# An S4 convolution block on one core: K's transform kept by contiguous channels, and two FFT stages turned through DRAM

## The chip, the cores and the metric

The kernel runs on one core of a Trainium2 chip. The metric is the device time of one execution in microseconds. Engines are named as in the profile: PE (TensorE matmul), PEld (its weight load), DVE (VectorE), ACT (ScalarE), POOL (GpSimd) and SP (SyncE, which issues most DMAs).

## What is computed

```python
mod = (silu(c) @ w_mod).reshape(1, 6, 1, 512)
sa, ca, ga, sb, cb, gb = (mod[:, i] for i in range(6))
h = layernorm(x) * (1 + ca) + sa                  # x: (1, 2048, 512)
x = x + ga * s4(h)                                # long convolution along the sequence
h = layernorm(x) * (1 + cb) + sb
x = x + gb * (mish(h @ w1 + b1) @ w2)             # 512 -> 1792 -> 512

def s4(u):
    P = exp((dt * A)[:, :, None] * arange(2048))  # A: (512 channels, 128 states), complex
    K = einsum("dn,dnl,dn->dl", C, P, dt * B).real
    y = irfft(rfft(u padded to 4096) * rfft(K padded to 4096))[:2048]
    return y + u * Dskip
```

Everything is float32. The feed-forward part runs as products of high and low parts, three matmuls for one.

## The kernel before

**The convolution as two-stage transforms.** The 2048 rows of the sequence are read as 128 x 16 (a partition holds 16 consecutive rows, index j), the 512 channels as four blocks b of 128. A transform has an outer stage (small matrices bdk, bdu for the input, di for the way back) and an inner stage (128 x 128 matrices mf forward, mi back, 32 of them). Both are matmuls, and between the stages data has to be turned, since a matmul contracts over partitions. A block's work is cut into eight groups v = 8b + s; 32 groups in all.

**The K branch** makes the convolution kernel for 16 channels per group. Angles (`s_ang`, one two-bank PSUM tile `pang`), rounding (`s_ri`) and its subtraction on PE (`s_neg`), sine and cosine (`s_sin`) and magnitudes (`s_mag`, L377, L380) meet in `s_comb` on DVE (L387 to L391); `s_kgen` multiplies them on PE (L402), `s_ks` adds the skip term, `s_ka` runs the outer stage (weights ks, moving bdk, L418) and `s_tm` copies it to the one tile `gk` (L426), in an order of channels that differs between even and odd blocks. `s_ubk` takes its weights from gk with a stride (L546, tile `pkb`): for a fixed group and r, neighbouring channels are 16 or 128 bytes apart.

**The u branch** per block: `h_slice` loads the block's rows again and normalises them on ACT (L512; block 0 uses the rows `XR` that are already in SBUF); `ua` runs the outer stage with h's slices as weights and bdu as the moving operand (L526), so channels come out on partitions, and scales by 1 + ca (L528, `modp[:, 3]`); `s_ut` turns them with PE transposes (L536) and copies to `gu` (L538); `s_ubu` runs the inner stage with gu as weights and adds the shift sa (rows `sab`, made by `shift_mm` and `shift_rows`) through a short bf16 matmul (L553); `s_ug` scales by ga (L563).

**Product and way back.** `s_prod` multiplies both spectra on DVE, channels on partitions (L583 to L585); `s_t1` transposes (L590, L592); `s_invb` runs the inner inverse with the data as weights (L601) and copies scattered to `z` (L603); `s_t2` transposes z (L611) into `zt` (L614); `s_inva` runs the outer inverse with the constant di as weights (L637), adds x (`s_xp` loads it) and stores to `x2d` in DRAM (L640).

**Order.** The work is a software pipeline over slots k = -1 to 40. `ORDER` lists the steps with an offset: a step with offset o does group k - o in slot k. `UD` adds a further offset per group to ua, ut, ubu and ug. `MS`, `SL` and `HS0` place the modulation vectors, parameters and row slices; `PRI0` and `PRI` move steps within a slot. From these priorities each engine gets a fixed instruction order; engines are in order and wait on each other by semaphores. SP's queue is in order as well: a DMA that waits for a buffer holds up those behind it. At slot 34 the generator's memory is released and w1 loaded (`mlp_open`), at the end the second layer norm (`ln_stats`, `ln_norm`, `ln_t`) hands over to the feed-forward loop (L897, L915).

Of the kernel before, what the change touches and what calls it, by code (L numbers as in the profile page):

```python
# [30 lines left out]
SL = {"p2": 0, "p3": 2, "ls0": 5, "raw": 2, "p0": 5, "ls1": 8, "co0": 6, "vis": 6, "h0": -5, "h1": -2}  # L31
HA = 4
NUG = 2
MS = [[3, 0], [5, 2], [0, 4], [1, 6], [2, 8], [4, 9]]
BN = [0, 0, 0, 1]
NS = 1
HS0 = [2, 3, 3, 2]
# [9 lines left out]
UD = [4, 4, 3, 3, 2, 3, 3, 3, 3, 3, 3, 3, 3, 3, 3, 4, 4, 4, 4, 4, 4, 4, 4, 4, 4, 4, 4, 4, 4, 4, 4, 4]  # L47
# [7 lines left out]
def _constants():  # L55
# [34 lines left out]
    for e in range(3):  # L90
# [12 lines left out]
        "bdk": bdk.reshape(P, 256).astype(f),  # L103
        "bdu": np.ascontiguousarray(bdu).reshape(P, 256).astype(f),
        "di": np.ascontiguousarray(di.transpose(1, 2, 3, 0, 4, 5)).reshape(P, 256).astype(f),
# [7 lines left out]
def _channels():  # L113

    d = np.arange(NB * P).reshape(NB, P)
    return np.stack([d[b].reshape(8, 2, 8).transpose(1, 0, 2) if b % 2 == 0 else
                     d[b].reshape(2, 8, 8).transpose(0, 2, 1) for b in range(NB)])
# [3 lines left out]
def s4_block(ctx, tc, io, out):  # L121
# [290 lines left out]
    def s_ka(k):  # L412
        p = bank("pka")
        PKA[k] = p
        for m in range(4):
            o = 256 * (m % 2) + 128 * (m // 2)
            for cc in range(2):
                T.matmul(p[64 * cc:64 * cc + 64, o:o + 128], KS[k][:, 64 * m:64 * m + 64],  # L418
                         bdk[:, 128 * cc:128 * cc + 128], start=True, stop=True)

    def s_tm(k):
        b, c = divmod(k, 8)
        if k == 0:
            GK[0] = big.tile([P, 8, 16, 8, 4], F32, tag="gk", name="gk")
        dst = GK[0][:, c] if b % 2 == 0 else GK[0][:, :, :, c, :].rearrange("p s d e -> p d s e")
        A.copy(dst, PKA[k].rearrange("p (d s e) -> p d s e", d=16, s=8))  # L426
# [5 lines left out]
    modp = keep.tile([P, 5, NB], F32, name="modp")  # L432
# [4 lines left out]
    mcol = gen.tile([P, 20, KB], F32, name="mcol", bufs=1)  # L437

    def mod_load(n):
        s, k = divmod(n, KB)  # L440
        w = cv.tile([P, D], F32, tag="zt", name=f"wm{n}", bufs=4)
        nc.sync.dma_start(w, w_mod((2, 3, 4, 1, 5, 0)[s] * D, D, k))
        WM[n] = w
# [19 lines left out]
    PM = []  # L463

    def shift_mm(k):
        if k == 0:
            PM.append(bank("pmod"))
        T.matmul(PM[0], sc[:, k:k + 1].to_broadcast([P, P]), WM[20 + k], start=(k == 0), stop=(k == KB - 1))

    def shift_rows():  # L470
        p = PM[0]
# [6 lines left out]

# [19 lines left out]
    HS, XP, U1, GU, YY, YT, Z, ZT = {}, {}, {}, {}, {}, {}, {}, {}  # L498

    def h_slice(b, part):  # L500
        if part == 0:
            HS[b] = sl8(f"h{b}").rearrange("p (j d) -> p j d", j=16)
            if b > 0:
                for j4 in range(4):
                    x_rows(HS[b][:, 4 * j4:4 * j4 + 4], 4 * j4, 4, b)
            return
        h = HS[b]
        bs = slice(b * P, b * P + P)
        for jj in range(4 * (part - 1), 4 * part):
            src = XR[jj][:, bs] if b == 0 else h[:, jj, :]  # L510
            if jj % 4 < HA:
                A.activation(h[:, jj, :], src, AF.Identity, scale=rstd[:, jj:jj + 1], bias=nmr[:, jj:jj + 1])  # L512
            else:
                V.tensor_scalar(h[:, jj, :], src, mv[:, jj, 0:1], rstd[:, jj:jj + 1],
                                op0=OP.subtract, op1=OP.mult)

    def s_ua(n):
        for j4 in ((0,), (1,), (2, 3), ())[n % 4]:
            ua(n // 8, n % 8 // 4, j4)

    def ua(b, rp, j4):
        if j4 == 0:
            U1[b, rp] = cv.tile([P, 8, 16, 16], F32, tag="u1", name=f"u1_{b}_{rp}")
        p = bank("pua")
        for jj in range(4):
            T.matmul(p[:, 128 * jj:128 * jj + 128], HS[b][:, 4 * j4 + jj, :],  # L526
                     bdu.rearrange("p (a r) -> p a r", r=32)[:, :, 16 * rp:16 * rp + 16], start=True, stop=True)
        A.mul(U1[b, rp][:, :, 4 * j4:4 * j4 + 4, :].rearrange("p a j r -> p j a r"),  # L528
              p.rearrange("p (j a r) -> p j a r", j=4, a=8), modp[:, 3, b:b + 1])

    def s_ut(v):
        b, s = divmod(v, 8)
        u = U1[b, s // 4].rearrange("p a j r -> p (a j) r")
        p = bank("put")
        for r in range(4):
            T.transpose(p[:, P * r:P * r + P], u[:, :, 4 * (s % 4) + r], ident)  # L536
        GU[v] = cv.tile([P, 4, P], F32, tag="gu", name=f"gu{v}")
        A.copy(GU[v].rearrange("p r d -> p (r d)"), p)  # L538
# [463 lines left out]
```

## Time and profile before

| | us |
|---|---|
| median of three runs | 763.28 |
| lowest and highest | 763.0, 764.53 |
| span of the profiled execution | 758.2 |
| PE busy, of the span | 707.0 |
| DVE busy | 450.6 |
| ACT busy | 428.3 |
| first feed-forward matmul (L897) at | 437.9 |

The span runs from the first to the last instruction; the runs' times also hold what lies around it, and no time outside the span is given for the profiled execution itself. A PE record is one pass of a matmul: a float32 matmul of the convolution part leaves two. Busy times of groups overlap, because matmuls are pipelined, so that groups add up to more than PE's busy time in a window; the chain that ended last counts each moment once.

### The profile page before, as it was taken

The page shows a single profiled execution, that of the slowest core. Times are in us where ns is not written, and L with a number is a line of the kernel's source. Part 1 is how long each engine was busy: PE and PEld are TensorE (multiplying, and loading weights), DVE is VectorE, ACT ScalarE, POOL GpSimd, SP SyncE. Part 2 cuts the span into 40 slices and gives each one's busy share as a digit, 9 for nine tenths or more (in the row PEclk, how much of TensorE's full clock was granted, in tenths as well). Part 3 has the DMA queues.
Part 4 walks back from the last instruction along what each step waited for, and adds up shares of the span by engine and source line. Part 5 has one row for each costly group of instructions (what it writes and reads, how often), then busy time and mean ns, then how long its engine had stood idle before and what let it go on. Part 6 is the DMA issues. An engine that isn't in the chain of part 4 may idle for free.

```text
span 758.2 us, 14266 instructions
## 1 busy us (share of the span) xinstructions
PE 707.0 (93%) x5888; PEld 587.0 (77%) x5888; DVE 450.6 (59%) x918; ACT 428.3 (56%) x689; POOL 52.4 (7%) x108
## 2 busy tenths in 40 slices
PE   0794999999999999999998789999999999999997
PEld 0562879987888898889888568888888888888885
DVE  6889798799899969984464487119211521143113
ACT  3767798989999998776664254233222322232221
POOL 1006203310060200000000000000000000000000
PEclk9987899999999999999999899999999999999999
DMA  9653224200241101110460362002200220002001
GB/s 312 237 194 77 63 66 116 48 8 10 58 112 57 43 2 43 57 57 2 148 215 28 97 187 65 0 1 92 75 1 1 81 87 1 0 1 84 0 1 55
DMA packets 47096, 52.70 MB, mean 70 GB/s; under 512 B 7221, under 2 KB 32825, under 8 KB 46265
## 3 DMA queue, kind: packets, MB, share of 16 engines
q1 hardware_dynamic: 40312, 47.93, 19.6%
q0 software_dynamic: 6720, 3.87, 2.7%
q8 instruction: 46, 0.75, 0.4%
q14 instruction: 18, 0.14, 0.1%
HBM read 41.30 MB, written 8.39 MB: 66 GB/s over the span
## 4 chain that ended last, share of the span: by engine, by line
PE 84%; DVE 7%; ACT 5%; DMA 2%; issue 1%; POOL 0%; SPq 0%; DVEq 0%; ACTq 0%; POOLq 0%
PE pm L897 20%; PE po L915 20%; PE pkb L546 8%; PE pka L418 4%; PE pub L546 4%; PE pua L526 4%; PE pib L601 4%; PE pkg L402 4%; PE pia L637 3%; PE put L536 2%; PE pang L344 2%; PE pang L362 2%; PE pmodp L448 2%; PE pt L611 2%; PE pt L590 2%; ACT ec L145 1%
## 5 line engine op out<-in xcount | busy, mean ns | idle before, releaser
L145 ACT ACTIVATE mh<-pm,b 128x512 f32<-128x512 f32 x56 | 38.6, 690 | 200.0 <-PE pm L897 200.0
L904 DVE TENSOR_TENSOR mal<-mh,mah 128x512 fp32r<-128x512 f32 x56 | 38.7, 691 | 177.6 <-ACT mah L903 177.3
L897 PE MATMUL pm<-hh,w1h 128*128 128x512 f32 x448 | 139.1, 393 | 2.8 <-ACT hh L803 2.8
L897 PEld LDWEIGHTS pm<-hh,w1h 128*128 128x128 f32 x448 | 84.5, 189 | 21.6 <-ACT hh L803 3.5
L915 PE MATMUL po<-w2h,mah 128*128 128x512 f32 x224 | 87.9, 392 | 0.0
L897 PE MATMUL pm<-hh,w1l 128*128 128x512 f32 x224 | 87.5, 392 | 0.0
L915 PE MATMUL po<-w2l,mah 128*128 128x512 f32 x224 | 87.5, 391 | 0.0
L915 PE MATMUL po<-w2h,mal 128*128 128x512 f32 x224 | 87.5, 390 | 0.0
L583 DVE TENSOR_TENSOR q<-pkb,ug 128x512 f32<-128x512 f32 x64 | 41.2, 685 | 47.4 <-PE pkb L546 47.3
L546 PE MATMUL pkb<-mf,gk 128*128 128x128 f32 x256 | 63.3, 389 | 0.2
L546 PEld LDWEIGHTS pkb<-mf,gk 128*128 128x128 f32 x256 | 60.6, 318 | 1.8 <-ACT gk L426 0.5
L603 ACT COPY z<-pib 128x512 f32<-128x512 f32 x32 | 35.1, 1098 | 33.7 <-PE pib L601 33.7
L897 PEld LDWEIGHTS pm<-hh,w1l 128*128 128x128 f32 x224 | 42.5, 190 | 8.8
L915 PEld LDWEIGHTS po<-w2h,mal 128*128 128x128 f32 x224 | 42.1, 188 | 8.6
L915 PEld LDWEIGHTS po<-w2h,mah 128*128 128x128 f32 x224 | 42.1, 188 | 8.4
L915 PEld LDWEIGHTS po<-w2l,mah 128*128 128x128 f32 x224 | 42.1, 188 | 8.2
L387 DVE TENSOR_TENSOR ec<-ec,m 128x1024 f32<-128x1024 f32 x32 | 38.9, 1216 | 9.8 <-ACT ec L145 9.8
L402 PE MATMUL pkg<-ec 128*32 128x64 f32 x2048 | 40.8, 228 | 0.5 <-DVE ec L388 0.3
L526 PE MATMUL pua<-bdu,h 128*128 128x128 f32 x256 | 37.5, 286 | 3.2 <-ACT h L512 3.2
L402 PEld LDWEIGHTS pkg<-ec 128*32 128x32 f32 x2048 | 34.4, 112 | 7.3 <-issue 2.2
L418 PE MATMUL pka<-bdk,ks 128*64 128x128 f32 x512 | 39.5, 289 | 0.1
L377 DVE TENSOR_TENSOR m<-co 128x1024 f32<-128x1024 f32 x32 | 38.9, 1216 | 0.1
(167 smaller groups left out, 1322.5 us busy)
## 6 DMA issues: line engine op xcount, KB each, us to landing
wm<-in_w_mod SPq DMA_DIRECT2D x24, 256.0 KB, 3.1
xr<-in_A_u SPq DMA_DIRECT2D x4, 1024.0 KB, 12.9
out<-ot SPq DMA_DIRECT2D x16, 256.0 KB, 2.0
xp<-in_A_u SPq DMA_DIRECT2D x15, 256.0 KB, 3.0
x2d<-xp SPq DMA_DIRECT2D x15, 256.0 KB, 2.4
xt<-x2d SPq DMA_DIRECT2D x15, 256.0 KB, 4.5
w1s<-in_B_w SPq DMA_DIRECT2D x8, 448.0 KB, 4.0
w2s<-in_B_w SPq DMA_DIRECT2D x14, 256.0 KB, 2.9
```

Of the source, the lines that this page charges most:

```text
L145: chain(A.activation(out, in_, f, **kw))
L377: V.tensor_mul(m2.rearrange("p d (a b) -> p d a b", a=8), co[:, :, 12:20, None].to_broadcast([P, 16, 8, 8]), co[:, :, None, 20:28].to_broa ...
L387: V.tensor_mul(ec[:, :, :, 32:64], ec[:, :, :, 95:63:-1], m2[:, None, :, 0:32].to_broadcast([P, 2, 16, 32]))
L402: T.matmul(o, ec[:, z, e, 0:32], ec[:, z, e, 32:96], start=(z == 0), stop=(z == 1))
L418: T.matmul(p[64 * cc:64 * cc + 64, o:o + 128], KS[k][:, 64 * m:64 * m + 64], bdk[:, 128 * cc:128 * cc + 128], start=True, stop=True)
L526: T.matmul(p[:, 128 * jj:128 * jj + 128], HS[b][:, 4 * j4 + jj, :], bdu.rearrange("p (a r) -> p a r", r=32)[:, :, 16 * rp:16 * rp + 16], s ...
L546: T.matmul(pv[:, :, r, :], lh(r), mf[:, 4 * s + r, :].rearrange("p (c s) -> p c s", c=2), start=not started, stop=True, skip_group_check=s ...
L583: V.tensor_mul(q, kv[:, c, :, None, :].to_broadcast([P, 4, 2, 64]), ug)
L603: A.copy(Z[b, hf][:, :, :, o:o + 4].rearrange("p j a r -> p r a j"), p.rearrange("p (r a j) -> p r a j", r=4, a=8))
L897: T.matmul(p, w1[wi][:, k, fs], hh[:, hi, k, :], start=(n == 0), stop=(n == 3 * KB - 1))
L904: V.tensor_sub(a[1], h, a[0])
L915: T.matmul(PO[tt][q], a[ai][:, P * q:P * q + P], w2[wi][:, f, :], start=(f == 0 and n == 0), stop=(f == FB - 1 and n == 2))
```

## The change

- `s_ka` writes its result with r outside and four channels inside, into places that interleave the 16 channels; `s_tm` copies them so that `gk` holds, for every r, 128 contiguous channels. There is one gk tile per block now, odd and even blocks in different memory. `bdk` and the order of channels on the host (`_channels`) follow.
- The outer input stage runs once for all channels, early (slots 1 to 4): DVE normalises the rows in place, 512 channels at a time (`norm`, 16 of them); `ua` takes the constant bdu as weights and a row group as the moving operand, 512 columns, 16 j x 2 halves. ACT copies to a staging tile, and pairs of j are stored to a DRAM tile `ud`. `s_gl` loads a group's `gu` from there, turned, in place of `s_ut`. The second read of the rows (`h_slice`) goes.
- The factor 1 + ca moves behind the stage: `s_ug` scales by gd = ga (1 + ca), and the shift is divided by 1 + ca (`shift_ratio`). The shift's rows come from a column form, made like the other modulation vectors, and four small broadcast matmuls.
- `s_invb` takes the constant mi as weights and the data as the moving operand; the result is copied contiguously and stored to DRAM tiles `zd`; `s_zl` loads it back turned, in place of the transposes of `s_t2`.
- `UD` goes; offsets, some buffers' tags and the places of the modulation vectors change. Tiles `gu` and the modulation weights share four buffers; `us` stages both ud and z in two.

```diff
-SL = {..., "vis": 6, "h0": -5, "h1": -2}
-MS = [[3, 0], [5, 2], [0, 4], [1, 6], [2, 8], [4, 9]]
+SL = {..., "vis": 6}
+MS = [[3, 0], [5, 1], [0, 3], [1, 6], [2, 8], [4, 9]]
+MR = 5
-UD = [4, 4, 3, 3, 2, ...]
 ORDER = [
-    ("kgen", 1), ("ks", 1), ("ubu", 3), ("ang", -2), ("ua", -1), ("hs", 0), ("ri", -2), ("misc", 0),
-    ("t2", 13), ("mag", -1), ("t1", 9), ("ka", 1), ("par", 0), ("tm", 1), ("neg", -2), ("ut", 2),
-    ("comb", 0), ("ubk", 8), ("inva", 13), ("ug", 4), ("xp", 10), ("sin", -2), ("invb", 9), ("prod", 8),
+    ("kgen", 1), ("ks", 1), ("ubu", 7), ("ang", -2), ("gl", 6), ("ri", -2), ("misc", 0), ("zl", 13),
+    ("mag", -1), ("t1", 9), ("ka", 1), ("par", 0), ("tm", 1), ("neg", -2),
+    ("comb", 0), ("ubk", 8), ("inva", 14), ("ug", 7), ("xp", 13), ("sin", -2), ("invb", 9), ("prod", 8),
 ]
...
     def s_ka(k):
+        pv = p.rearrange("p (r d) -> p r d", d=16)
         for m in range(4):
-            o = 256 * (m % 2) + 128 * (m // 2)
+            o = 8 * (m % 2) + 4 * (m // 2)
             for cc in range(2):
-                T.matmul(p[64 * cc:64 * cc + 64, o:o + 128], KS[k][:, 64 * m:64 * m + 64],
+                T.matmul(pv[64 * cc:64 * cc + 64, :, o:o + 4], KS[k][:, 64 * m:64 * m + 64],
                          bdk[:, 128 * cc:128 * cc + 128], start=True, stop=True)

     def s_tm(k):
-        dst = GK[0][:, c] if b % 2 == 0 else GK[0][:, :, :, c, :].rearrange("p s d e -> p d s e")
-        A.copy(dst, PKA[k].rearrange("p (d s e) -> p d s e", d=16, s=8))
+        if c == 0:
+            GK[b] = (cv if b % 2 else big).tile([P, 32, P], F32, tag="gk", name=f"gk{b}", bufs=1)
+        A.copy(GK[b][:, :, 16 * c:16 * c + 16], PKA[k].rearrange("p (r d) -> p r d", d=16))
...
+    def shift_ratio():
+        d = modp[:, 3, :]
+        V.tensor_scalar(gd, d, 0.0, 1e-20, op0=OP.is_equal, op1=OP.mult)
+        V.tensor_add(d, d, gd)
+        V.tensor_mul(gd, modp[:, 0, :], d)
+        V.reciprocal(d, d)
+        V.tensor_mul(modp[:, 5, :], modp[:, 5, :], d)
...
     def shift_rows():
+        for b in range(NB):
+            T.matmul(p[:, b * P:b * P + P], modp[:, 5, b:b + 1].to_broadcast([P, P]), ident, start=True, stop=True)
...
+    def norm(j):
+        V.tensor_scalar(XR[j], XR[j], mv[:, j, 0:1], rstd[:, j:j + 1], op0=OP.subtract, op1=OP.mult)
+
+    def ua(j, hf):
+        if j % 2 == 0:
+            US[j // 2, hf] = cv.tile([P, NB, 2, P], F32, tag="us", name=f"us{j}{hf}", bufs=2)
+        t = US[j // 2, hf]
         p = bank("pua")
+        T.matmul(p, bdu[:, P * hf:P * hf + P], XR[j], start=True, stop=True)
+        A.copy(t[:, :, j % 2, :], p.rearrange("p (b d) -> p b d", b=NB))
+        if j % 2:
+            nc.sync.dma_start(view(ud, hf * NB * P * SEG + (j - 1) * P, [[SEG, P], [P * SEG, NB], [1, 2 * P]]),
+                              t.rearrange("p b j d -> p b (j d)"))
+
+    def s_gl(v):
         b, s = divmod(v, 8)
+        GU[v] = cv.tile([P, 512], F32, tag="gu", name=f"gu{v}", bufs=4).rearrange("p (r d) -> p r d", r=4)
+        nc.sync.dma_start(GU[v], view(ud, (s // 4 * NB + b) * P * SEG + 4 * (s % 4) * 8 * SEG,
+                                      [[P, P], [8 * SEG, 4], [1, P]]))
...
     def s_ubk(v):
+        kr = lambda r: GK[b][:, 4 * s + r, :]
...
     def s_invb(v):
         for r in range(4):
-            T.matmul(p[:, P * r:P * r + P], YT[v][:, r, :], mi[:, 4 * s + r, :], start=True, stop=True)
+            T.matmul(p[:, P * r:P * r + P], mi[:, 4 * s + r, :], YT[v][:, r, :], start=True, stop=True)
+        z = cv.tile([P, 4, P], F32, tag="us", name=f"z{v}", bufs=2)
+        A.copy(z, p.rearrange("p (r d) -> p r d", r=4))
+        nc.sync.dma_start(view(zd[b][s // 4], 4 * (s % 4) * 8 * SEG, [[P, P], [8 * SEG, 4], [1, P]]), z)
+
+    def s_zl(y):
+        ZT[b, j4] = cv.tile([P, 2, 512], F32, tag="x4", name=f"zt{b}{j4}", bufs=3)
+        for hf in range(2):
+            nc.sync.dma_start(ZT[b, j4][:, hf, :].rearrange("p (j d) -> p j d", j=4),
+                              zd[b][hf][:, 4 * j4:4 * j4 + 4, :])
...
+    at(MR, shift_ratio)
+    at(MR, shift_rows)
...
+    for n, j in enumerate((12, 13, 14, 15, 8, 9, 10, 11, 0, 1, 2, 3, 4, 5, 6, 7)):
+        at(NS, norm, j)
+        for hf in range(2):
+            at(NS + n // 4, ua, j, hf)
```

More of the change, by code (lines that the diff above doesn't have):

```diff
@@ L497, in s4_block @@
     LNX, LST = {}, {}
[L498 to L523, printed above, removed]
-        p = bank("pua")
[L525 to L529, printed above, removed]
@@ L531, in s_ut @@
-    def s_ut(v):
-        b, s = divmod(v, 8)
[L533 to L538, printed above, removed]
+    XP, GU, YY, YT, ZT, US = {}, {}, {}, {}, {}, {}
+    SEG = 16 * P
+    ud = dram.tile([2 * NB * P, SEG], F32, name="ud")
+    zd = [[dram.tile([P, 16, P], F32, name=f"zd{b}{hf}") for hf in range(2)] for b in range(NB)]
```

104 lines of the change are left out of this document (33 added, 71 removed).

## The prediction

> **What bounds the kernel now.** I read the page first, then the busy time by stage, then the chain that ended last.
>
> ```profile
> span 758.2 us, 14266 instructions
> ...
> PE 707.0 (93%) x5888; PEld 587.0 (77%) x5888; DVE 450.6 (59%) x918; ACT 428.3 (56%) x689; POOL 52.4 (7%) x108
> ...
> PE   0794999999999999999998789999999999999997
> ...
> DVE  6889798799899969984464487119211521143113
> ACT  3767798989999998776664254233222322232221
> ```
>
> PE is at 9 from the sixth slice to the end, but DVE and ACT stand at 8 and 9 too until slice 17. The change touches nothing after the first feed-forward matmul (437.9 us), so the question is what stands behind PE before that. I cut the span there: parameters, head (36 us, first combination of a channel group, to 109, the ninth), steady stage (to 347, where the 32nd and last group's combination ends), drain (to 420, last inverse), hand-over. The columns of the next view are the window, its length, the busy us of PE, PEld, DVE, ACT and POOL with counts, the granted clock, DMA share and GB/s.
>
> ```profile
> 0.00:36.00 36.00, 13.93 (x48) 10.29 (x48) 27.30 (x108) 18.77 (x36) 2.81 (x12) 1.00 0.83 288
> 36.00:109.00 73.00, 59.33 (x749) 44.54 (x749) 64.14 (x139) 58.10 (x103) 16.59 (x32) 0.86 0.33 97
> 109.00:347.00 238.00, 236.52 (x3073) 205.41 (x3074) 205.18 (x339) 211.57 (x338) 33.01 (x64) 0.99 0.19 51
> 347.00:420.00 73.00, 69.55 (x576) 60.58 (x576) 34.94 (x61) 43.93 (x68) 0.00 (x0) 0.99 0.33 105
> 420.00:438.00 18.00, 13.36 (x49) 8.47 (x50) 10.93 (x45) 3.72 (x7) 0.00 (x0) 0.85 0.32 102
> ```
>
> In the steady stage PE is busy 236.5 of 238 us; DVE (205.2) and ACT (211.6) come close behind. In the drain PE is alone: 69.6 of 73 against 34.9. In the head nobody is full and DVE is nearest (64.1 of 73).
>
> **What PE loses.** Shares of the span on the chain that ended last, by line, then the page's row that also names L611:
>
> ```profile
> by line: PE pm L897 19.7%; PE po L915 19.6%; PE pkb L546 7.7%; PE pka L418 4.4%; PE pub L546 3.8%; PE pua L526 3.6%; PE pib L601 3.6%; PE pkg L402 3.5%; PE pia L637 3.0%; PE put L536 2.1%; PE pang L344 2.0%; PE pang L362 1.9%; PE pmodp L448
> ...
> PE pm L897 20%; PE po L915 20%; PE pkb L546 8%; PE pka L418 4%; PE pub L546 4%; PE pua L526 4%; PE pib L601 4%; PE pkg L402 4%; PE pia L637 3%; PE put L536 2%; PE pang L344 2%; PE pang L362 2%; PE pmodp L448 2%; PE pt L611 2%; PE pt L590 2%; ACT ec L145 1%
> ```
>
> A share times 758.2 us by the line's records in the whole run (8 for each of 32 groups, 256, for pkb, pub and pua, as 176 in the stage and 80 in the drain show below for pkb; 4 for each, 128, for put and L611) gives the time that one record holds PE: pkb 58.4/256 = 0.228 us, pub 28.8/256 = 0.113, pua 27.3/256 = 0.107, put 15.9/128 = 0.124, L611 15.2/128 = 0.118. pkb and pub run the same number of matmuls of one shape; only the weights' layout differs, strided in gk, contiguous in gu. The change makes gk contiguous, so I price pkb like pub: 0.115 less per record. Bounds: 0 (the layout isn't the cause) to that. The steady stage holds these counts, out of PE's and ACT's groups:
>
> ```profile
> L546 PE MATMUL pkb<-mf,gk 128*128 128x128 f32 x176 | 43.0, 386 | 0.1
> L526 PE MATMUL pua<-bdu,h 128*128 128x128 f32 x176 | 24.2, 275 | 0.0
> L536 PE MATMUL put<-ident,u 128*128 128x128 f32 x92 | 14.7, 284 | 0.0
> L611 PE MATMUL pt<-ident,z 128*128 128x128 f32 x72 | 11.0, 273 | 0.0
> L603 ACT COPY z<-pib 128x512 f32<-128x512 f32 x21 | 23.3, 1111 | 14.1 <-PE pib L601 14.1
> L512 ACT ACTIVATE h<-h,nmr,rstd 128x128 f32<-128x128 f32 x48 | 20.9, 492 | 0.0
> L528 ACT ACTIVATE u<-pua,modp 128x512 f32<-128x512 f32 x23 | 15.9, 699 | 1.0 <-PE pua L526 0.7
> L538 ACT COPY gu<-put 128x512 f32<-128x512 f32 x23 | 13.8, 604 | 0.4 <-PE put L536 0.4
> L592 ACT COPY yt<-pt 128x512 f32<-128x512 f32 x21 | 12.5, 596 | 0.3 <-PE pt L590 0.3
> ```
>
> PE loses 176 x 0.115 = 20.2 (pkb), 176 x 0.107 = 18.8 (pua, moved to the head), 92 x 0.124 = 11.4 and 72 x 0.118 = 8.5 (transposes): 58.9, so 177.6 stay. ACT loses h, u and gu (50.6), and the z copy, scattered now and contiguous then, falls to yt's price (21 x 0.515 = 10.8): at most 150 stay. DVE loses nothing. So **DVE with its 205.2 us becomes the bound of the steady stage**: 205 if it never waits, 228 if it is 90% busy. I take 95%, 216: DVE is in order and waits on ACT and PE chains at least a little. Stage: -22, bounds -33 and -10.
>
> One edit here has no row: pka now writes runs of 4 floats, 64 bytes apart, in place of 128 in a row. The nearest row is pub, which writes two runs of 64 at pka's own pace, so I price it at nothing; if it doubled, its 4.4% of the span would be 33 us more on PE, 24 of them in this stage (23 of 32 groups), and PE's 202 would stand beside DVE's 205. The Trainium skill (Advanced Engine Details and Errata, PSUM Cachelines) says that non-contiguous PSUM patterns slow matmuls significantly, and that two consecutive elements want to be contiguous: by its first sentence the stage would be some 10 us longer than I say, by its second not; no row here shows runs this short.
>
> **The head.** Here work is added. The outer input stage for all channels runs as 16 x 2 matmuls of 512 columns, 64 records like pia's (0.107 for 128 columns makes 0.43 for 512): 27.5 us, against 8.8 (pua) and 0.7 (put) that leave. The rows are normalised at full width on DVE, 16 instructions like L790, which is 8.6 us, plus five tiny ones (0.8) for the shift's ratio; 32 ACT copies at 0.60 replace h, u and gu. The shift's four broadcast matmuls turn into 16 column matmuls and four small ones, about even: 5.2 us now, then 32 records like L448's (10.7/80 = 0.134 each) and 8 like put's, 5.3. First three groups of PE in the head, then two of the whole run, then three times of single instructions:
>
> ```profile
> L526 PE MATMUL pua<-bdu,h 128*128 128x128 f32 x48 | 8.8, 337 | 3.2 <-ACT h L512 3.2
> L468 PE MATMUL pmod<-wm,sc 128*128 128x512 f32 x8 | 5.2, 742 | 0.0
> L448 PE MATMUL pmodp<-sc,wm 128*128 128x1 f32 x80 | 10.7, 260 | 0.0
> ...
> L637 PE MATMUL pia<-zt,di 128*128 128x512 f32 x64 | 30.4, 605 | 0.0
> L790 DVE TENSOR_SCALAR xt<-xt,mv,rst 128x512 f32<-128x512 f32 x16 | 8.0, 539 | 0.1
> ...
> 71.12 0.16 DVE L489 SCALAR_TENSOR_TENSOR rstd<-rsq,rstd 128x16 f32<-128x16 f32 x1
> ...
> 104.06 1.16 PE L546 MATMUL pub<-mf,gu 128*128 128x128 f32 x8
> ...
> 427.29 0.32 SPq L640 DMA_DIRECT2D x2d<-xt  x1
> ```
>
> DVE: 64.1 + 9.4 = 73.5 busy, with its 8.9 us of idle as now 82.4, +9. PE: 59.3 + 27.5 - 9.5 = 77.3, under that. The staging tile has two buffers: one pair of rows costs four ACT copies (2.4), an issue (0.32, L640) and a store's landing (2.4, in the rows on the hand-over), 5.1 us. Eight pairs take 41, from the finished scales (71.3, the end of L489) to 112; with the turned load's landing (3.0, like xp's) that is 115, where the first pub is at 104 now. So the products start 11 us late, at about the delay that DVE has anyway, and cost nothing more unless ACT, queued behind a staging wait, holds up the sines. Bounds 0 (everything in today's idle) and +22; I take +9.
>
> **The drain.** Its rows, PE's and then DVE's:
>
> ```profile
> L546 PE MATMUL pkb<-mf,gk 128*128 128x128 f32 x80 | 20.2, 396 | 0.1
> L611 PE MATMUL pt<-ident,z 128*128 128x128 f32 x40 | 6.0, 273 | 0.0
> L536 PE MATMUL put<-ident,u 128*128 128x128 f32 x32 | 5.2, 285 | 0.0
> L526 PE MATMUL pua<-bdu,h 128*128 128x128 f32 x32 | 4.6, 275 | 0.0
> ...
> L583 DVE TENSOR_TENSOR q<-pkb,ug 128x512 f32<-128x512 f32 x20 | 12.9, 685 | 28.9 <-PE pkb L546 28.9
> ```
>
> PE loses 9.2 + 4.7 + 4.0 + 3.4 = 21.3 and keeps 48.3. Twenty L583 are ten products: PE is two groups late today. With DVE as the pace there are eight left, 8/10 x 48.3 = 39, plus some 3 us until the last is through. The added DMA is in the way a little: besides today's 7.7 MB (105 GB/s in 73 us) about six turned loads, eight stores and eight loads back, 0.26 MB each, 13.5 MB together; at the first window's full rate (288/0.83 = 347 GB/s) 39 us. I take 45, -28; bounds -21 (ten products still) and -36.
>
> **The hand-over.** Times of four instructions:
>
> ```profile
> 419.38 1.01 ACT L603 COPY z<-pib 128x512 f32<-128x512 f32 x1 [1.56 <-PE pib L601]
> 420.45 3.68 PE L611 MATMUL pt<-ident,z 128*128 128x128 f32 x16 [1.10 <-ACT z L603]
> 423.92 7.76 PE L637 MATMUL pia<-zt,di 128*128 128x512 f32 x16
> 437.86 1.22 PE L897 MATMUL pm<-hh,w1h 128*128 128x512 f32 x4 [2.10 <-ACT hh L803]
> ```
>
> ```profile
> xp<-in_A_u SPq DMA_DIRECT2D x15, 256.0 KB, 3.0
> x2d<-xp SPq DMA_DIRECT2D x15, 256.0 KB, 2.4
> ```
>
> From the last z copy to pia 4.5 us pass. Then: copy 0.6, store 2.4, load 3.0, three issues 1.0: 7.0, nothing beside it. I take +3 (2.5 and a little for the queue), bounds +1 and +8 (the loads queued behind one another). Elsewhere the round trip through DRAM is covered: a turned load is issued one slot (about 9 us) ahead of pub, the load back 1.4 slots ahead of pia. The four new streams carry 1024 x 2048 floats each, 33.5 MB; the steady stage's part, some 25 MB in 216 us, is 116 GB/s, a third of the full rate on top of a share of 0.19.
>
> **Sum.** +9 - 22 - 28 + 3 = -38 on the span of 758.2, so 720; the median of the runs, 763.3, lies 5.1 above the span, so **725**. With all bounds together it is 695 (0 - 33 - 36 + 1) and 762 (+22 - 10 - 21 + 8).
>
> **Rivals.** (a) The pace of the steady stage isn't set by an engine's sum. The angles have one PSUM buffer: pang, bias, rounding, negation, Abs, Sin go round once per group over three in-order engines. If that or the table switches hold it at 10.35 us per group (238/23), the stage gives 0, the drain -21 (PE no longer late matters less): +9 - 21 + 3 = -9, **754**. For it: DVE idles 33 us in the stage already; against: with PE at 178 and ACT at 150 of 238 each hop of that round waits less than today. (b) The slower side: the turn through DRAM stays exposed. SP is one in-order queue; stores of z wait there for ACT, loads back wait for stores, and the turned load for the next pub stands behind them, with the product behind pub on DVE. With a wait of w us per group, in 23 groups of the stage and 8 of the drain, the sum is 31w + 9 + (207 - 238) - 28 + 3 = 31w - 47: slower from w = 1.5, and with a store's landing each time (2.4) +27, **790**. Against it speaks the slot of lead. (c) PE falls out of full clock. In the head PE is busy 81% and the granted clock averages 0.86; the steady stage would be 82% busy. At 0.86 the 177.6 are 206 and still hide; at 0.67, 265 us, the drain 60: +9 + 27 - 13 + 3, **789**. It decides below about 0.72. The Trainium skill (TensorE: Matmul & The Clock Gate, HAM oscillation) puts the limit at PE gaps of about 3.4 us; by that rule (c) doesn't happen, since about 1.7 us of idle per group remains, in several gaps. The head's lowered clock goes with a PE wait of 3.2 us at pua (its row above), so the trace doesn't contradict it. (d) The strided weights aren't why pkb is slow: PE keeps 198, still under DVE; the drain gives 9 less, **734**, inside the forecast.
>
> **Chances.** Forecast (DVE-paced, 695 to 744): 0.62, (a) 0.22, (b) 0.09, (c) 0.07. About 0.2% (1.5 us) is what a measurement tells from no change; of (a) 0.03 falls within it. Faster 0.81, same 0.03, slower 0.16. The range 702 to 760 leaves out (b) and (c) and a few hundredths below.
>
> **What would show it.** Right: pkb's mean near pub's 287 ns and its weight loads near 190; DVE busy 95% in the steady stage with PE near 80%; the last L391 at about 335, the last inverse near 380, the first L897 matmul near 400; clock near 1.0. Wrong: DVE waiting long for pub or pkb with PE idle (b); PE clock under 0.8 (c); the same 10.35 us between groups (a); the first pub later than 125 us (head over its bound).

## The result, and the profile after

| | us |
|---|---|
| changed kernel, median of 4 runs (lowest to highest) | 754.69 (749.49 to 757.51) |
| kernel before, 4 runs beside it | 763.72 (763.0 to 764.53) |
| ratio with its 95% interval | 0.9883 [0.9839, 0.9926] |
| profiled execution of the changed kernel: time, span | 749.49, 747.7 |

The change gains 9 us where 38 were forecast; the profiled execution gains 10.5 on the span. All times here and below leave out one execution, of e6, that ran at a granted clock of 0.75 and took 871.7 us. The prediction's windows are cut again by the same landmarks: start of the first combination of a group (L388 of the changed kernel, L391 before), of the ninth, of the last, the last z copy, the first feed-forward matmul. All "heads" and "stages" below are measured like this, from each kernel's profiled execution:

| us | before | forecast | after | step |
|---|---|---|---|---|
| up to the first combination | 36.2 | 36 | 39.4 | +3.2 |
| head (first to ninth combination) | 72.6 | +9 | 106.6 | **+34.0** |
| steady stage (ninth to last) | 238.0 | -22 | 208.5 | -29.5 |
| drain (to the last z copy) | 72.7 | -28 | 51.7 | -21.0 |
| hand-over (to the first feed-forward matmul) | 18.5 | +3 | 20.2 | +1.7 |
| feed-forward part | 320.4 | 0 | 321.3 | +0.9 |

Three of the four forecast steps came within their bounds. The head took 25 us more than its forecast. The 3.2 us before the first combination were not forecast and stay unexplained. The windows of the changed kernel, with the same columns as in the prediction (window, length, busy us of PE, PEld, DVE, ACT and POOL with counts, granted clock, DMA share, GB/s):

```profile
39.00:147.00 108.00, 83.26 (x808) 53.72 (x807) 75.10 (x171) 64.67 (x114) 16.50 (x32) 0.84 0.48 152
147.00:356.00 209.00, 192.52 (x2847) 155.82 (x2842) 201.15 (x327) 156.08 (x232) 32.43 (x64) 0.99 0.47 130
356.00:406.00 50.00, 41.98 (x343) 33.87 (x342) 30.91 (x60) 22.48 (x35) 0.00 (x0) 0.98 0.72 223
406.00:424.00 18.00, 11.37 (x33) 4.79 (x32) 8.62 (x32) 1.21 (x2) 0.00 (x0) 0.87 0.63 193
```

In the steady stage DVE is now busy 201.2 of 209 us (96%): the bound moved from PE to DVE, as forecast. In the head nobody is full: PE 83.3 of 108, DVE 75.1, ACT 64.7. Next, three of PE's groups on the page of the changed kernel (mean ns of one behind the comma, then idle time before it and its releaser):

```profile
L512 PE MATMUL pua<-xr,bdu 128*128 128x512 f32 x64 | 31.6, 642 | 13.6 <-DVE xr L505 13.1
L416 PE MATMUL pka<-bdk,ks 128*64 128x128 f32 x512 | 39.8, 286 | 3.4 <-DVE ks L405 3.4
L530 PE MATMUL pkb<-mf,gk 128*128 128x128 f32 x256 | 37.8, 284 | 1.8 <-ACT gk L423 1.8
```

pkb fell from 389 to 284 ns, to pub's price. pka, whose output now goes to PSUM in runs of 4 floats, stays at 286 ns (289 before). The outer stage's 64 records are there with 31.6 us, and with a wait of 13.1 us for the normalised rows. How that wait looks on PE and on ACT, in the timeline of each engine in the head (start, length, what; idle time before it in brackets):

```profile
73.84 3.78 PE L512 MATMUL pua<-xr,bdu 128*128 128x512 f32 x4 [12.70 <-DVE xr L505]
78.06 6.08 PE L512 MATMUL pua<-xr,bdu 128*128 128x512 f32 x12 [0.44 <-DVE xr L505]
84.06 1.17 PE L399 MATMUL pkg<-ec 128*32 128x64 f32 x64
```

```profile
75.95 0.58 ACT L513 COPY us<-pua 128x512 f32<-128x512 f32 x1 [13.65 <-PE pua L512]
...
84.09 1.07 ACT L513 COPY us<-pua 128x512 f32<-128x512 f32 x2 [2.77 <-DMA ud<-us]
86.56 1.07 ACT L513 COPY us<-pua 128x512 f32<-128x512 f32 x2 [1.39 <-DMA ud<-us]
87.52 0.39 ACT L404 COPY ks<-pkg 128x256 f32<-128x256 f32 x1
87.78 1.06 ACT L364 ACTIVATE ec<-pang 128x1024 f32<-128x1024 f32 x1
88.70 1.06 ACT L142 ACTIVATE ec<-pang 128x1024 f32<-128x1024 f32 x1
```

PE stands for 12.7 us and ACT for 13.7 us until the rows are normalised, while work of the generator stands behind the outer stage's instructions in their queues: on PE the products of a combination (L399, at 84.06), on ACT the angles and their sines (L364 and L142, from 87.78, without any wait of their own by then). The groups are counted off by their records, 64 of L399 each: the products at 84.06 are those of the second group. DVE's timeline shows the last instruction of that group's combination at 49.01, so that it ended at 50.2, and that of the fourth group (L386, ended at 70.8) before the last scales (L490) were done:

```profile
49.01 1.22 DVE L388 TENSOR_TENSOR ec<-ec,m 128x1024 f32<-128x1024 f32 x1
...
70.15 0.69 DVE L386 SCALAR_TENSOR_TENSOR ec<-ec,m 128x512 f32<-128x512 f32 x1
...
72.96 0.17 DVE L490 SCALAR_TENSOR_TENSOR rstd<-rsq,rstd 128x16 f32<-128x16 f32 x1
73.24 2.87 DVE L505 TENSOR_SCALAR xr<-xr,mv,rstd 128x512 f32<-128x512 f32 x6
```

So the products of the second group came 34 us after its combination. In PE's queue they stand behind the first 16 outer matmuls, and each following group's products stand behind 16 more (PE's timeline again):

```profile
99.50 7.11 PE L512 MATMUL pua<-xr,bdu 128*128 128x512 f32 x16
...
107.34 1.17 PE L399 MATMUL pkg<-ec 128*32 128x64 f32 x64
...
109.92 7.11 PE L512 MATMUL pua<-xr,bdu 128*128 128x512 f32 x16
```

The products of the second, third and fourth group thus ran 34, 31 and 37 us after their combinations; in the kernel before it was 0.5, 0.1 and 6.4 us. Meanwhile these three groups filled the three buffers of the tile `ec` (`bufs=3` at L343 of the changed kernel), so that a fifth group could not be begun: its sines (87.78) and its combination (90.81) came only after the second group's products had ended (85.2).

The waits of the head and the chain of work in it tell the same from the other side:

```profile
ACT us L513 <- PE pua L512: 18.9, 7, 13.7
DVE ec L384 <- ACT ec L142: 16.9, 3, 11.4
...
PE pua L512 <- DVE xr L505: 13.1, 2, 12.7
ACT us L513 <- DMA ud<-us: 11.6, 6, 3.2
```

```profile
by line: PE pua L512 21.2%; PE pmodp L445 9.5%; PE pka L416 7.9%; ACT ec L142 5.5%; PE pkg L399 5.4%; DMA ud<-us 4.8%; DVE xr L505 4.3%; issue 3.9%; PE pang L341 3.8%; ACT ec L364 3.7%; DVE ec L388 3.2%; PE pang L359 2.4%; DVE m L374 2.1%; 
```

pua holds 21% of the head's chain, the most of any line, and DVE's combination waits 16.9 us for ACT's sines (L142). The wait of ACT for the store of a staging tile (11.6 us) is the second candidate. Experiments e1 to e3 ask which of the two sets the head.

### The profile page after: what moved, and what is told of

Its sections match the earlier page's. It is cut to its first block, busy times and chain, and to the rows that moved or that the text cites. A ratio compares the mean times of both kernels' runs of the same rounds, so it can differ in the third digit from the quotient of the medians.

```text
span 747.7 us, 13563 instructions
## 1 busy us (share of the span) xinstructions
PE 659.3 (88%) x5472; PEld 517.5 (69%) x5472; DVE 455.7 (61%) x940; ACT 358.4 (48%) x565; POOL 51.7 (7%) x108
## 4 chain that ended last, share of the span: by engine, by line
PE 69%; DVE 16%; DMA 7%; ACT 6%; issue 1%; POOL 0%; SPq 0%; DVEq 0%; ACTq 0%; POOLq 0%
PE pm L868 20%; PE po L886 19%; PE pka L416 3%; PE pua L512 3%; PE pkg L399 3%; PE pub L530 3%; PE pkb L530 3%; PE pmodp L445 2%; PE pib L579 2%; PE pia L614 2%; DVE ec L388 2%; PE pang L341 2%; DVE q L564 2%; DVE ec L384 2%; PE pang L359 1%
## 5 line engine op out<-in xcount | busy, mean ns | idle before, releaser
L142 ACT ACTIVATE mh<-pm,b 128x512 f32<-128x512 f32 x56 | 38.5, 690 | 202.7 <-PE pm L868 202.7
L384 DVE TENSOR_TENSOR ec<-ec,m 128x1024 f32<-128x1024 f32 x32 | 39.0, 1219 | 20.0 <-ACT ec L142 19.8
L399 PE MATMUL pkg<-ec 128*32 128x64 f32 x2048 | 40.2, 228 | 4.5 <-DVE ec L388 4.5
L512 PE MATMUL pua<-xr,bdu 128*128 128x512 f32 x64 | 31.6, 642 | 13.6 <-DVE xr L505 13.1
L399 PEld LDWEIGHTS pkg<-ec 128*32 128x32 f32 x2048 | 34.4, 112 | 11.6 <-issue 7.3
L364 ACT ACTIVATE ec<-pang 128x1024 f32<-128x1024 f32 x32 | 32.9, 1027 | 15.0 <-PE pang L359 14.8
L530 PE MATMUL pkb<-mf,gk 128*128 128x128 f32 x256 | 37.8, 284 | 1.8 <-ACT gk L423 1.8
L388 DVE TENSOR_TENSOR ec<-ec,m 128x1024 f32<-128x1024 f32 x32 | 38.9, 1217 | 0.0
```

Source lines behind the costliest of these rows:

```text
L142: chain(A.activation(out, in_, f, **kw))
L384: V.tensor_mul(ec[:, :, :, 32:64], ec[:, :, :, 95:63:-1], m2[:, None, :, 0:32].to_broadcast([P, 2, 16, 32]))
L388: V.tensor_mul(ec[:, :, :, 0:32], ec[:, :, :, 0:32], m1[:, None].to_broadcast([P, 2, 16, 32]))
L399: T.matmul(o, ec[:, z, e, 0:32], ec[:, z, e, 32:96], start=(z == 0), stop=(z == 1))
L512: T.matmul(p, bdu[:, P * hf:P * hf + P], XR[j], start=True, stop=True)
L530: T.matmul(pv[:, :, r, :], lh(r), mf[:, 4 * s + r, :].rearrange("p (c s) -> p c s", c=2), start=not started, stop=True, skip_group_check=s ...
```

## The experiments

The table gives what the runs measured; "ratio" is against the kernel before, run on the same chip. Head, stage and drain come from one profiled execution each. Kernels that leave out a part of the work, and so do not compute the block, ran once ("one run"). e11 is e6's kernel, run once more for its profile (742.8 us): in their row time and ratio are e6's, the stages e11's.

| run | time, us | ratio [95%] | head | stage | drain |
|---|---|---|---|---|---|
| e1, outer stage: matmuls only | 748.7 | one run | 108.0 | 206.6 | 52.4 |
| e2, outer stage: copies and stores only | 747.4 | one run | 89.7 | 224.9 | 51.8 |
| e3, four staging tiles | 751.1 | 0.9892 [0.9855, 0.9928] | 107.1 | 210.3 | 52.9 |
| e4, outer stage later | 743.6 | 0.9783 [0.9722, 0.9843] | 99.7 | 211.0 | 51.0 |
| e7, later, four staging tiles | 746.2 | 0.9824 [0.9761, 0.9886] | 99.5 | 209.4 | 51.6 |
| e8, e7 with earlier statistics | 738.5 | 0.9704 [0.9641, 0.9766] | 88.4 | 213.2 | 50.2 |
| e12, e8 with the normalisation in four parts | 736.8 | 0.9681 [0.9650, 0.9712] | 88.3 | 214.9 | 51.0 |
| e14, e12 with unread matmuls in PE's gaps | 736.7 | 0.9685 [0.9629, 0.9741] | 90.6 | 209.7 | 51.8 |
| e17, e12 with modulation vectors a slot later | 737.9 | 0.9717 [0.9655, 0.9779] | 86.7 | 216.2 | 53.1 |
| e5, no outer stage | 737.6 | one run | 88.6 | 215.4 | 51.1 |
| e9, nor normalisation | 730.1 | one run | 81.4 | 216.0 | 51.6 |
| e13, e9 with unread matmuls | 729.2 | one run | 83.9 | 212.4 | 52.6 |
| e16, e9 with modulation vectors a slot later | 725.3 | one run | 73.3 | 216.9 | 52.8 |
| e6 and e11, K's layout and the turn of z, u as before | 739.3 | 0.9699 [0.9641, 0.9758] | 75.3 | 218.4 | 68.9 |
| e15, the turn of z alone | 758.7 | 0.9980 [0.9950, 1.0011] | 74.3 | 233.5 | 71.7 |
| e10, constant weights and the turn per block | 749.9 | 0.9861 [0.9816, 0.9907] | 85.9 | 216.2 | 64.5 |

**Which leg of the outer stage sets the head (e1, e2, e3).** e1 leaves out copies and stores, e2 leaves out the matmuls, e3 gives each row index its own staging tile, four of them.

```diff
 e1, in ua (and s_gl reads raw rows):
-        A.copy(t[:, :, j % 2, :], p.rearrange("p (b d) -> p b d", b=NB))
-        if j % 2:
-            nc.sync.dma_start(...)
 e2, in ua:
-        p = bank("pua")
-        T.matmul(p, bdu[:, P * hf:P * hf + P], XR[j], start=True, stop=True)
-        A.copy(t[:, :, j % 2, :], p.rearrange("p (b d) -> p b d", b=NB))
+        A.copy(t[:, :, j % 2, :], XR[j].rearrange("p (b d) -> p b d", b=NB))
 e3, in ua:
-        t = US[j // 2, hf]
+        t = cv.tile([P, NB, P], F32, tag="us", name=f"us{j}{hf}", bufs=4)
```

> Leaves out the outer input stage's 32 ACT copies and 16 stores (the turned loads read the raw rows instead); its 64 matmul records and the normalisation stay. In the changed kernel the ninth combination starts at 146.0 us, before at 108.7. Theory A (the stage's matmuls, 27.5 us on the in-order PE after the late row scales, hold up the generator): it stays late, 132 to 145. Theory B (ACT, in order, waits for staging buffers and stores in front of the sines): it falls to 105 to 118.

> Leaves out the outer input stage's matmuls; ACT copies the normalised rows themselves to the staging tile, with all stores and the normalisation. Theory A: the ninth combination falls to 110 to 120. Theory B: it stays at 132 to 145.

> Four staging tiles of 2 KB in place of two of 4 KB, a store per row group. Theory A: the ninth combination moves by at most 5 us (the share of the store landings on the head's chain), total 750 to 756. Theory B: it falls by the 11.6 us of ACT's waits for stores or more, total 740 to 745.

Without copies and stores the head stays at 108.0 (106.6 with them); without the matmuls it falls to 89.7. So the matmuls and their wait set the ninth combination, and staging doesn't: four tiles leave the head at 107.1 and the ratio at 0.989. The products of the second to fourth group say the same: they run 36, 30 and 36 us after their combinations in e1, and 7, 1 and 2 us in e2. e2's ninth combination still came at 127.3, later than the 110 to 120 that were expected. And in e2 the last combination came no earlier (352.1, against 354.5 after and 352.6 in e1), since the stage took 224.9. The chain of e2 up to the ninth combination shows the other leg:

```profile
by line: DMA ud<-us 17.4%; PE pmodp L445 15.5%; ACT us L511 11.9%; PE pka L416 10.8%; PE pkg L399 7.5%; PE pang L341 6.0%; ACT ec L142 4.7%; ACT ec L364 4.3%; PE pang L359 4.0%; issue 3.8%; DMA gu<-ud 3.4%; ACT gk L423 1.9%; ACT L145 1.5%; 
```

Stores and ACT copies now hold 29% of it. The first product of the spectra on DVE starts at 149.8 us with this leg alone (e2), at 153.7 with the matmuls alone (e1) and at 156.7 with both. The two legs end within 4 us of each other, so taking one away shows little in the total: 6.0 us in e1 and 7.3 in e2, but 17.1 in e5 below, without either.

**Moving the stage (e4, e7, e8, e12).** e4 gives the outer matmuls and copies a later place within the slot and moves them all a slot on; e7 adds e3's tiles; e8 also gets the statistics and row scales ready earlier; e12 normalises four rows a slot instead of 16 at once.

```diff
 e4:
-PRI0 = {..., "ua": 0.008, ...}
+PRI0 = {..., "ua": 0.9, ...}
-            at(NS + n // 4, ua, j, hf)
+            at(NS + 1 + n // 4, ua, j, hf)
 e8, beside e7's:
-BN = [0, 0, 0, 1]
+BN = [0, 0, 0, 0]
+PRI0 = {"st": -0.4, "no": -0.4, "nr": -0.3, ...}
 e12, beside e8's:
-        at(NS, norm, j)
+        at(NS + n // 4, norm, j)
```

> The outer input stage one slot later (slots 2 to 5) and behind the generator's steps within a slot. Theory A: the generator's matmuls go first, DVE idles less, the ninth combination comes at 120 to 135, total 735 to 748, unless the first turned load is then late by as much. Theory B: the copies are behind the sines and wait behind nothing, much the same, so this run alone doesn't tell A from B; if nothing moves, the stage's place isn't the cause.

> e4 (outer stage one slot later, behind the generator in a slot) together with e3 (four half-size staging tiles). Theory A2: with both legs eased the gain is more than e4's and e3's together (7 and 0 to 3 us): ninth combination 120 to 130, total 728 to 740. Theory C: no better than e4, 742 to 746.

> e7 with the statistics and the row scales ahead of the generator's steps of their slots, so that the outer stage's rows are ready sooner and its matmuls fall into PE's idle time of the head (17 us between 39 and 72). Theory A2: 4 to 10 us better than e7. Theory C: within 3 us of e7, or worse, since DVE's generator steps are put off.

> e8 with the normalisation in four blocks, each in the slot ahead of its matmuls, in place of one. Theory D: PE's idle stretch and the half clock after it shrink, 3 to 8 us better than e8, 728 to 736. Rival E: the same work, within 2 us of e8.

The same work in another order takes 18 us from the head (106.6 to 88.4 in e8) and brings the whole to 0.9704. The later place alone takes 6.9 of them (e4), the earlier statistics the other 11.1 (e8 against e7): in e4 the products of the third and fourth group still run 22 and 28 us after their combinations, in e8 1 and 6 us. The ninth combination came later than expected in e4 (138.8, expected 120 to 135) and e7 (137.2, expected 120 to 130). The four staging tiles add nothing here either (e7 against e4), and spreading the normalisation adds nothing that the intervals can tell (0.9681 against 0.9704).

**What the head is made of (e5, e9, e16, e17).** e5 leaves the outer stage out, e9 also the normalisation; e16 also puts two modulation vectors and the shift's rows a slot later, where the kernel before has them.

```diff
 e5, in ua (and s_gl reads raw rows):
+        return
 e9, beside e5's:
-        at(NS, norm, j)
 e16, beside e9's (e17: beside e12's):
-MS = [[3, 0], [5, 1], [0, 3], [1, 6], [2, 8], [4, 9]]
-MR = 5
+MS = [[3, 0], [5, 2], [0, 4], [1, 6], [2, 8], [4, 9]]
+MR = 6
```

> Leaves out the outer input stage altogether (matmuls, copies, stores); the turned loads read the raw rows at once, the normalisation stays on DVE. e1 and e2 each removed one leg and left the end of the generator at 352. Theory A2 (two legs of nearly the same length, PE's matmuls and the copy-and-store chain, together hold up head and first products; the rest of the prediction holds): ninth combination at 108 to 120, last one at 315 to 330, total 715 to 730. Theory C (something else, as the modulation loads in the shared gu buffers or DVE's sum of work, sets the end of the generator): last combination stays above 340, total above 738.

> e5 without the normalisation as well (the 16 DVE instructions are left out). e5's ninth combination is still at 126.6, 18 us after the kernel before, with PE's clock at 0.60 between 72 and 121 us. Theory D (the block of 16 normalisations holds the generator's DVE steps for 7.5 us, PE falls idle for 4.5 us there and runs at half clock after it, so that the head pays twice): the ninth combination falls by 12 us or more, to 108 to 115, and the clock of that stretch rises above 0.8. Rival E (only its own 7.5 us): 118 to 121, clock as in e5.

> The kernel without outer stage and normalisation (both left out: the turned loads read raw rows, so the values are not the reference's), with two modulation vectors and the shift rows back one slot later, at the places of the kernel before. Without this its head (first to ninth combination) took 81.4 us, against 72.6 before. Theory G1: what is left of the head's growth is the modulation work, moved one slot forward into the slots of the first groups: the head falls by 4 to 9 us, to 72 to 77. Rival G2: it is the rest of the order (statistics all on DVE queue places, other priorities, turned loads): the head stays within 79 to 84.

> The complete kernel with the normalisation in four blocks and the outer stage later (0.968 of the kernel before; head 88.3 us), with the same two modulation vectors and the shift rows one slot later. Theory G1: head 80 to 85, time 730 to 734, ratio 0.958 to 0.963. Rival G2: head 87 to 91, ratio 0.965 to 0.972.

The head falls from 106.6 to 88.6 (outer stage, 18.0), 81.4 (normalisation, 7.2, its DVE time of 7.5) and 73.3 (places of the modulation vectors, 8.1), which is the 72.6 of before within a microsecond. e5 had promised more (the ninth combination at 108 to 120, measured 126.6): the outer stage is only half of the head's growth. The parts hold for this order of taking them away: in the complete kernel (e17) the later modulation vectors shortened the head by only 1.6 us (88.3 to 86.7) and the total not at all, a miss for the theory that had been right in e16. What holds the head in their place there is not shown.

**The granted clock (e13, e14).** In e9 PE's clock averaged 0.73 in the head, so a slow PE was the rival to the order of work. Six bf16 matmuls a slot in slots 1 to 8, read by nobody, were put into PE's gaps.

```diff
+    for i in range(6):
+        def warm():
+            T.matmul(bank("pw"), su[:, 0, 0:P], su[:, 0, :], start=True, stop=True)
+        for k in range(1, 9):
+            at(k, warm)
```

> e9 (no outer input stage, no normalisation) plus 48 bf16 matmuls of 512 columns whose result nobody reads, six in each of slots 1 to 8, to keep PE busy. e9's head is still 9 us longer than the one before although PE and DVE have less to do; PE's clock is 0.69 between 72 and 121 us. Theory F (the emptier PE runs at half clock, so each generator matmul in the loop of waits takes twice as long): the clock rises above 0.85, the head falls from 81 to 72 to 77 us. Rival G (the order of instructions holds it): the head stays at 80 or grows by part of the 48 x 0.2 to 0.4 us added.

> e12 with the same 48 filling matmuls. Theory F: clock in the head up, 2 to 8 us better than e12, 729 to 735. Rival G: 738 to 748, the added work is paid on PE, which the outer stage fills anyway.

The head of e9, then of e13 (the granted clock is the last number but two):

```profile
38.00:119.00 81.00, 66.47 (x820) 53.81 (x821) 63.30 (x144) 52.62 (x88) 16.75 (x32) 0.73 0.35 101
```

```profile
38.00:121.00 83.00, 69.83 (x859) 50.57 (x860) 62.34 (x143) 52.82 (x88) 17.17 (x32) 0.84 0.33 96
```

and the same two for e12 and e14:

```profile
39.00:127.00 88.00, 80.31 (x793) 55.50 (x795) 70.14 (x155) 61.37 (x106) 17.04 (x32) 0.86 0.64 182
```

```profile
39.00:127.00 88.00, 82.62 (x814) 53.73 (x814) 70.59 (x160) 59.76 (x101) 16.64 (x32) 1.00 0.63 177
```

The clock rose from 0.73 to 0.84 and from 0.86 to 1.00, and the heads became no shorter (81.4 to 83.9, 88.3 to 90.6; e14's total is e12's, which neither theory had expected). The lowered clock goes along with the gaps; nothing here shows it to set the head's length. The unread matmuls take PE time themselves (PE is busy 3.4 and 2.3 us more), so a gain of that size could be hidden.

**The parts alone (e6, e11, e15, e10).** e6 and e11 are the kernel before with the new layout of gk and the new way back of z, and nothing changed in the u branch; e15 is the kernel before with the way back of z alone; e10 keeps the constant weights and the turn of u through DRAM, but block by block, spread over the slots as before. K's layout alone is not among the runs: the second gk tile takes 16 KB of each partition, and these are free only once the turn through DRAM has replaced the two z tiles of 8 KB.

```diff
 e6, e11 and e15, against the kernel before:
-            T.matmul(p[:, P * r:P * r + P], YT[v][:, r, :], mi[:, 4 * s + r, :], start=True, stop=True)
+            T.matmul(p[:, P * r:P * r + P], mi[:, 4 * s + r, :], YT[v][:, r, :], start=True, stop=True)
 e6 and e11 besides:
+            o = 8 * (m % 2) + 4 * (m // 2)
+        kr = lambda r: GK[b][:, 4 * s + r, :]
 e10, in ua, against the changed kernel:
+        for jj in range(4):
+            T.matmul(p[:, P * jj:P * jj + P], bdu[:, P * hf:P * hf + P], HS[b][:, 4 * j4 + jj, :], start=True, stop=True)
+        t = cv.tile([P, 512], F32, tag="us", name=f"us{b}{hf}{j4}", bufs=4)
```

> The kernel before with two parts of the change alone: K's layout and the inverse's turn through DRAM; the u branch is as before (rows normalised per block on ACT, outer stage per block, PE transposes). Theory A2: head as before (ninth combination 106 to 114), steady stage 222 to 232 us since PE keeps 30 us more than in the changed kernel, drain 52 to 60, total 735 to 745. Theory C: total 750 or more, since the head wasn't the loss.

> e6's kernel again for its profile. Theory A2: PE is the bound of the steady stage once more, over 97% busy, and takes 222 to 232 us; head under 80 us from the first to the ninth combination. Rival C: the head is as long as in the changed kernel.

> The kernel before with the inverse's turn through DRAM alone (K's layout and the u branch as before). By the prediction's prices PE loses the transposes of z, 8.5 us in the steady stage and 4.7 in the drain, ACT their copies: steady stage 226 to 232, total 748 to 756, and e6's further gain (739) is K's layout. Rival (K's layout isn't why pkb is slow, the gain of e6 is the turn): 738 to 745, pkb's weight loads near 190 ns though K is as before.

> The changed kernel with the outer input stage spread again: per block of 128 channels as before (rows read again and normalised on ACT), but with bdu as the constant weights, the result stored to DRAM and loaded turned. No full-width normalisation on DVE, the same number of PE columns in all, a quarter of them in the head. Theory A2 with D (the head's loss is the stage's being done all at once): ninth combination 108 to 118, steady stage 208 to 220 (DVE still the bound), drain 50 to 55, total 718 to 732. Rival C (something else of the change holds the head or the end of the generator): total 735 or more.

The turn of z alone brings nothing that can be told from no change (0.998 [0.995, 1.0011]; 748 to 756 us were expected): the stage gains 4.5 us, and head and hand-over take most of it back. With K's layout beside it the ratio is 0.9699. The weight loads of pkb (count, busy, mean ns) in e15 and in e11:

```profile
L548 PEld LDWEIGHTS pkb<-mf,gk 128*128 128x128 f32 x256 | 60.8, 318 | 1.6 <-issue 0.5 <-ACT gk L426 0.2
```

```profile
L547 PEld LDWEIGHTS pkb<-mf,gk 128*128 128x128 f32 x256 | 33.1, 197 | 1.8 <-issue 0.5 <-ACT gk L425 0.2
```

318 ns a load with the strided weights, 197 with contiguous ones. K's layout is all that separates the two kernels, and their intervals lie apart: it is what gained, from 0.998 to 0.970. The other operations that the layout touches keep their price: a copy into gk takes 598 ns in e15 and 604 in e11, a record of pka 290 and 294; pkb falls from 390 to 282. The drain of e15 says why the turn of z gave so little there:

```profile
345.00:417.00 72.00, 67.80 (x560) 58.80 (x551) 35.40 (x64) 33.86 (x56) 0.00 (x0) 0.98 0.59 181
```

PE is still busy 67.8 of 72 us (69.6 of 73 before): the transposes that left were a small part of a drain still bound by PE, and the hand-over grew by 2.3 us. e6 came to 739.3 us, inside its 735 to 745, but partly by luck: the stage was shorter than its 222 to 232 (218.4) and the drain longer than its 52 to 60 (68.9). Drains near 52 were seen only in the kernels that do the outer stage of u at once, or leave it out. e10 missed (718 to 732 us expected, 749.9 measured): its head (85.9) is shorter than the changed kernel's, but the drain stayed at 64.5. Ten products are left in it where the changed kernel has nine, PE still runs 32 records of the outer stage (4.1 us), and DVE waits 12.9 us for pkb (5.4 in the changed kernel); what delays pkb there stays open.

## Why the prediction was wrong

**The step that failed is the head's term**, "DVE: 64.1 + 9.4 = 73.5 busy, with its 8.9 us of idle as now 82.4, +9", with "PE: 59.3 + 27.5 - 9.5 = 77.3, under that" and "cost nothing more unless ACT, queued behind a staging wait, holds up the sines". It measured +34.0, beyond its bound of +22. Two things were wrong in it.

First, busy sums over the whole 73 us were compared with its length, as if the added work could go anywhere. It can't: the row scales end at 73.1 us (71.3 before), and the first outer matmul starts at 73.8. The 27.5 us on PE (31.6 measured) had the second half of the window only, in front of the generator's matmuls in PE's queue, and the wait for them stood on two in-order engines: 12.7 us of PE and 13.7 of ACT. The products of three groups came 31 to 37 us late for it, and with all buffers of `ec` full DVE had no group to go on with. The prediction worked out the staging cycle for itself and asked what was queued behind a staging wait; it did not ask what is queued on PE and ACT behind the first outer matmul. Taking the stage out gives 18.0 us back (e5), and as much comes from a later place with earlier statistics (e8, 18.2).

Second, one part had no price: the modulation vectors' move one slot forward. "About even" counts the matmuls of the shift alone; the place of the vectors cost 8.1 us in the kernel without outer stage and normalisation (e16 against e9), though only 1.6 in the complete one (e17 against e12). The normalisation was rightly in the +9 as busy time: it took 7.2 us of the head (e9), and it is busy for 7.5.

The condition named for a wrong prediction, "the first pub later than 125 us", came true: 141.1. The measured 754.7 us do lie in the outer range of 702 to 760, but only because that was drawn to take in rival (a); the forecast itself reached to 744.

**Steady stage, -22 forecast, -29.5 measured: right in its mechanism, off in size.** DVE is busy 96% (95% taken) and is the bound; pkb costs what pub costs, 284 ns; its weight loads take 191 ns, near the 190 named. PE is less relieved than thought (192.5 busy in 209, 92% where 80% were named). With the outer stage left out and the head short (e5, e9, e16) the stage takes 215 to 217 us, the 216 of the forecast (212.4 in e13). The 208.5 of the changed kernel go with its long head, which may give the steps behind it time to come nearer; no run shows that apart, so the 7.5 us beyond the forecast count as luck. The short PSUM runs of pka, priced at nothing, cost nothing: 286 ns against 289. The Trainium skill (Advanced Engine Details and Errata, PSUM Cachelines) had two readings: by its sentence on non-contiguous patterns pka would have become slower, by its sentence on two consecutive elements not; the trace agrees with the second.

**Drain, -28 forecast, -21.0 measured**: just at its bound of -21. Nine products were left when the last combination ended, one fewer than before and one more than the eight forecast, and DVE waits 5.4 us for pkb in it (28.9 before). **Hand-over, +3 forecast, +1.7 measured**, although the transfers were slower than their rows of before, as the landing times of the changed kernel show (KB each, median us):

```profile
ud<-us SPq DMA_DIRECT2D x16, 512.0 KB, 3.5
gu<-ud SPq DMA_DIRECT2D x32, 256.0 KB, 2.9
zd<-z SPq DMA_DIRECT2D x32, 256.0 KB, 2.6
zt<-zd SPq DMA_DIRECT2D x32, 256.0 KB, 4.1
x2d<-xp SPq DMA_DIRECT2D x15, 256.0 KB, 3.5
```

3.5 us for x2d's store (2.4 before) and 4.1 for a turned load of z (3.0 taken).

**The rivals.** (a) gave 754, which is the time that came out, but not for its reason: it said that a round over three engines keeps 10.35 us a group, and the pace is 208.5/23 = 9.07. The number agrees by accident, gained in the stage and lost again in the head. (b) is refuted: the waits of PE's weight loads for data on its way through DRAM in the steady stage come to 0.4 us in all:

```profile
PEld pia L614 <- DMA gu<-ud: 0.2, 1, 0.2
PEld pub L530 <- DMA zt<-zd: 0.2, 1, 0.2
```

(c) is refuted too: the clock in the stage is 0.99; where it was low, in the head, raising it gained nothing (e13, e14). (d) is refuted by e15 and e11: the strided weights were the cause of pkb's price.

**Where the gain went.** Stage and drain gave 50.5 us (29.5 + 21.0) and the head took 34.0 back, 18 of which the order cost (e8). With the order mended (e8, e12) the kernel stands at 0.968 to 0.970; the kernel with the old u branch (e6) stands at 0.970. The intervals overlap: the outer stage with constant weights, which goes with a shorter steady stage and drain, paid in its best form here about what it cost in the head. What else could make room in the head of the complete kernel stays open; e17 shows that the place of the modulation vectors isn't it.

## What to carry to other kernels

Work moved ahead of a pipeline is not priced by the idle time of a window: look up when its inputs are ready, count only the idle time behind that moment, and ask for each in-order engine that issues it what stands behind its first waiting instruction, and how soon the buffers in front of that are full. Before removing matmuls that transpose, look whether slow weight loads are the larger part: a strided weight operand shows in the profile as loads of 318 ns beside others of 190. When two legs of a stage end close together, leave out each in turn and judge by the end of the whole, not by the first landmark.

## What was not expected of the hardware

PSUM output in runs of four floats, 64 bytes apart, cost pka nothing (286 ns against 289). Weight loads with a stride between neighbouring channels took 318 ns against 191 for contiguous ones of the same shape. A higher granted clock in the head (1.00 in place of 0.86, with unread matmuls that took 2.3 us of PE themselves) made no difference to the time that the intervals can tell.
